# One Trainium2 core, attention and two MLPs: the first tile's output product taken in float32 on whole operands instead of three passes over split operands

## The chip, the core and the metric

The kernel runs on one core of a Trainium2 chip. That core has a matrix engine (TensorE; PE in the rows, with PEld for its weight loads), a vector engine (VectorE, DVE), a scalar engine (ScalarE, ACT), a general engine (GpSimd, POOL) and an engine that here only issues DMAs (SyncE, SP). Each works through its own queue in order, and semaphores tie the queues together. The metric is the device time of one execution in microseconds; lower is better.

## The reference

`reference` computes attention with a feature softmax on q and a sequence softmax on k (8 batches, 8 heads, 576 tokens, head size 64), then a gated MLP, then a second MLP:

```python
q_s = softmax over the head dimension of q
k_s = softmax over the sequence of k
attn = q_s @ (k_s.T @ v)                  # 8 x 8 x 576 x 64 -> x: 4608 x 512
xn = x / rms(x) * rms_g
g, val = xn @ w_gate, xn @ w_val          # 512 -> 1536
y = (silu(g) * val) @ w_out               # 1536 -> 512   <- the product that is changed, for the first 512 tokens
h = y @ w2_in; out = (h * sigmoid(1.702 * h)) @ w2_out    # 512 -> 2048 -> 512
```

q, k, v and rms_g arrive as float32. The five weight matrices arrive as float64 and are turned into float32 on the core.

## The kernel before

**Tiling.** The 4608 tokens are 9 tiles `j` of 512. The hidden width of the first MLP, 1536, is 12 chunks `n` of 128, the model width 512 is 4 chunks `c` of 128. Tile `j` runs through 36 slots, three for each hidden chunk `n`: slot 3n computes the gate product (`hidden`, 12 matmuls, then Silu on ScalarE at L828), slot 3n+1 the value product (`hidden`, 12 matmuls, then the multiplication `s = s * tv` on VectorE at L834), slot 3n+2 the output product `out1` of the chunk before, n-1.

**Split operands.** The products are made of three reduced-precision passes (dtype `float32r`): an operand is split into a high part and a remainder, and `product` (L490) issues high x high, high x low and low x high into the same accumulator. `split_u` (L507) makes the two parts of the gated values with two VectorE instructions, L509 (copy) and L510 (subtract). `split_weight` (L159) makes the two parts of a weight with one ScalarE instruction (L160) and one GpSimd instruction (L161).

**Weights in the first tile.** While tile 0 runs, each slot also calls `advance` once: it decodes one 128 x 512 piece of a float64 weight (ScalarE L148 and L149, VectorE L150, L151 and L154, GpSimd L157) and splits an earlier piece. Pieces of the gate and value weights are kept as their two parts. Pieces of `w_out` are kept whole (`weight["raw", n // 2]`), since they do not fit in both forms; `split_out_weight(n)` splits them again for every tile into a tile `wo`, in tile 0 in slot 3n+2, in the later tiles in slot 3n. The decoding of piece `w_out[n]` stands in slot 3n.

**What sets the order.** All instructions are recorded in program order under a manual schedule, and each engine executes its own in that order. `plan[j][slot]` adds the attention steps of the next tile (`unit_steps`), one unit of two heads every six slots: s0 is the maximum over k (VectorE L316), s1 and s2 transpose it twice on TensorE (L323, L335) with VectorE steps L327, L330, L336 between, s3 is the exponentials (ScalarE L354) and the row sums (VectorE L360 to L362, GpSimd L363), s4 the k-v product in plain float32 (TensorE L370, ten instructions) and its scaling (VectorE L378 to L385), then the q transposes (L399, L407, L408) and the attention products (L414 to L416). In slots 30 to 33 the norm of the next tile is made (`total` L449, `spread` L464, `scale` L470). From tile 1 on no slot calls `advance`.

After the nine tiles follow the two products of the second MLP (L639 and L984), which the change does not touch.

Of the kernel before, what the change touches and what calls it, by code (L numbers as in the profile page):

```python
# [20 lines left out]
def attention_glu_mlp(  # L21
# [26 lines left out]
    nc = tc.nc  # L48
# [4 lines left out]
    P = 128  # L53
# [4 lines left out]
    NC = DM // P  # L58
    NF1 = FF1 // P
# [52 lines left out]
    def f(x):  # L112
        return x.bitcast(F32)
# [51 lines left out]
    weight = {}  # L165
# [51 lines left out]
    def advance(limit=len(todo_pieces)):  # L217


        turn = at["decode"] < limit  # L220
        finish = decode_next() if turn else None
        if at["split"] < at["decode"] - (2 if turn else 0):
            split_next()
        if turn:
            if finish:
                finish()
            fetch_next()
# [3 lines left out]
    def decode_aside():  # L231

        if at["decode"] == len(todo_pieces):
            return
        piece = todo_pieces[at["decode"]]
        decode_next()()
        decoded.append((piece, halves.pop(piece)))
        fetch_next()

    def store_aside():  # L240
        if decoded:
            piece, w32 = decoded.pop(0)
            nc.sync.dma_start(out=w2_d[pieces2.index(piece)], in_=f(w32))
# [3 lines left out]
    def split_out_weight(n):  # L247
        w = sp.tile([P, 2, 512], F32R, tag="wr", bufs=2, name="wo")
        split_weight(w, f(weight["raw", n // 2][:, n % 2, :]))
        wo[n] = w  # L250
# [52 lines left out]
    def bank(tag):  # L303
        bufs = {"att": 2, "gv": 2, "acc": 4}[tag]
        return ps.tile([P, 512], F32, tag=tag, bufs=bufs, name=f"ps_{tag}")
# [175 lines left out]
    def split_x(j, c, side=nc.vector):  # L481
        x = xr.pop((j, c))
        w = sp.tile([P, 2, T], F32R, tag="xs", bufs=4, name="xs")
        nc.scalar.activation(w[:, 0, :], x, AF.Copy)
        side.tensor_tensor(w[:, 1, :], x, f(w[:, 0, :]), op=ALU.subtract)
        xs[j, c] = w
# [3 lines left out]
    def product(t, w, x, first, last):  # L490

        for i, (a, e) in enumerate(PASSES):
            nc.tensor.matmul(t, w(a), x(e), start=first and i == 0, stop=last and i == 2)  # L493

    def hidden(j, w):
        t = bank("gv")
        for c in range(NC):
            product(
                t,
                lambda a, c=c: w[:, a, c * P : (c + 1) * P],  # L500
                lambda e, c=c: xs[j, c][:, e, :],
                c == 0,
                c == NC - 1,
            )
        return t

    def split_u(s):  # L507
        u = sp.tile([P, 2, T], F32R, tag="u", bufs=2, name="u")
        nc.vector.tensor_copy(u[:, 0, :], s)  # L509
        nc.vector.tensor_tensor(u[:, 1, :], s, f(u[:, 0, :]), op=ALU.subtract)  # L510
        return u

    us, acc = {}, {}

    def out1(j, n):
        u, w = us.pop((j, n)), wo.pop(n)
        for c in range(NC):
            if n == 0:
                acc[c] = bank("acc")
            product(  # L520
                acc[c],
                lambda a: w[:, a, c * P : (c + 1) * P],
                lambda e: u[:, e, :],
                n == 0,
                n == NF1 - 1,
            )

    def store_x2(j, c):
        ev = sp.tile([P, T], F32, tag="ev", bufs=2, name="ev")
        nc.scalar.activation(ev, acc[c], AF.Copy)  # L530
        nc.scalar.dma_start(out=x2_d[j][c], in_=ev)
# [16 lines left out]
    def sums(raw, side, engines):  # L548
        for (o, a, b, op), engine in zip(SUMS[side], engines):
            engine.tensor_tensor(raw[:, o], raw[:, a], raw[:, b], op=op)  # L550
# [41 lines left out]
    def pack_steps(kind, q):  # L592
        a, b = (weight_steps(kind, 2 * q + i, nc.gpsimd) for i in range(2))
        return [a[0], b[0], a[1], b[1]] + [x for ab in zip(a[2:], b[2:]) for x in ab]
# [4 lines left out]
    def x2_load(i, c):  # L599
        raw = xraw2[i, c] = raw_tile()  # L600
        for k in range(4):
            done = 0
            while done < W:
                j, o = divmod((2 * i + k % 2) * W + done, T)
                n = min(W - done, T - o)
                nc.sync.dma_start(
                    out=raw[:, k, done : done + n], in_=x2_d[j][c + 2 * (k // 2)][:, o : o + n]
                )
                done += n

    def x2_split(i, p, c):
        pool, tag, bufs = (pools["x"], "xf", 12) if ORDER.index(p) < 5 else (pools["xb"], "xg", 4)
        w = pool.tile([P, 2, W], F32R, tag=tag, bufs=bufs, name=f"xf{p}{c}")
        halve(w[:, 0], w[:, 1], xraw2[i, c][:, RIGHT[p]], nc.vector)
        xfac[i, p, c] = w
# [114 lines left out]
    with tc.manual_schedule():  # L730
# [74 lines left out]
        for j in range(NTILE):  # L805
            if j + 1 == NTILE:

                ap.release()
                pools["raw"] = tc.alloc_tile_pool(name="r2", bufs=1, side="right", reuse_waits="tile")
                pools["x"] = tc.alloc_tile_pool(name="x2p", bufs=1, side="right", reuse_waits="tile")  # L810

                for q, gate in enumerate((10, 20)):
                    steps2 = pack_steps("2i", q)
                    todo += [(gate - 6, fn) for fn in steps2[:4]] + [(gate, fn) for fn in steps2[4:]]
                for c in range(2):
                    todo.append((0, lambda c=c: x2_load(0, c)))
                for c in range(2):
                    todo.append((28, lambda c=c: sums(xraw2[0, c], "B", (nc.vector,) * 4)))
                for p in ORDER[:5]:
                    for c in range(2):  # L820
                        todo.append((0, lambda p=p, c=c: x2_split(0, p, c)))

            for slot in range(SLOTS):
                n, part = divmod(slot, 3)
                if part == 0:
                    tg = hidden(j, weight["g", n])
                    s = sp.tile([P, T], F32, tag="s", bufs=2, name="s")
                    nc.scalar.activation(s, tg, AF.Silu)  # L828
                elif part == 1:
                    tv = hidden(j, weight["v", n])  # L830
                    if n == NF1 - 1 and j + 1 < NTILE:
                        for c in range(NC):
                            split_x(j + 1, c)
                    nc.vector.tensor_tensor(s, s, tv, op=ALU.mult)  # L834
                    us[j, n] = split_u(s)
                    if n == 1 and j:
                        for c in range(2, NC):
                            store_x2(j - 1, c)
                else:
                    if pend:  # L840
                        out1(*pend)
                    if n == 0 and j:
                        for c in range(2):
                            store_x2(j - 1, c)
                    pend = (j, n)
                for fn in plan[j][slot]:
                    fn()
                if part == (2 if j == 0 else 0):
                    split_out_weight(n)
                if j == 0:  # L850
                    advance(len(pieces1))
                elif j + 1 < NTILE:
                    if slot % 6 == 2:
                        decode_aside()
                    elif slot % 6 == 5:
                        store_aside()
                for _ in range(3 if slot < 33 else 2):
                    if todo and todo[0][0] <= slot:
                        todo.pop(0)[1]()
        out1(*pend)  # L860
        for c in range(NC):
            store_x2(NTILE - 1, c)
# [92 lines left out]
        for k in range(NT // T * NSET):  # L955
# [23 lines left out]
            for p in (1, 6, 7, 5, 3, 4, 2):  # L979
                w = wpack["2o", m // 2, p]  # L980
                t = banks[p]
                for i in range(2):
                    for n, (a, e) in enumerate(PASSES):
# [4 lines left out]
                            start=m == 0 and i == 0 and n == 0,  # L988
                            stop=last and n == 2,
# [84 lines left out]
```

## Time and profile before

| what | value |
|---|---|
| time, median of 3 runs | 1816.32 us (1816.26 to 1817.03) |
| time of the profiled execution | 1816.74 us |
| its span, first to last instruction | 1814.9 us |
| busy: PE, DVE, ACT, POOL | 1742.3, 1203.9, 779.9, 396.1 us |
| mean granted TensorE clock | 0.988 |

The span is 1.84 us shorter than the execution's own time; what lies around it is start and end. Shares of busy time are means over stages that have different limits. The first tile lies between about 43 and 204 us of the span; tiles 1 to 8 and then the second MLP fill the rest.

### The profile page before, as it was taken

How to read it: one execution, taken by the hardware profiler on the slowest of the kernel's cores; microseconds unless marked ns; L12 is line 12 of the kernel's file. 1: busy time of each engine (PE TensorE's matmuls, PEld its weight loads, DVE VectorE, ACT ScalarE, POOL GpSimd, SP SyncE). 2: the span in 40 equal slices, each digit the busy share in tenths (PEclk: the TensorE clock that was granted, in tenths of full speed). 3: DMA queues.
4: the chain of work that ended last, by engine and by line, in shares of the span. 5: the costliest groups of instructions: out<-in, count | busy, mean ns of one | idle time of the engine just before them, and what ended most of it. 6: DMA issues, size and time to landing. Idle time of an engine off the chain costs nothing.

```text
span 1814.9 us, 26699 instructions
## 1 busy us (share of the span) xinstructions
PE 1742.3 (96%) x10092; PEld 1543.3 (85%) x10092; DVE 1203.9 (66%) x2017; ACT 779.9 (43%) x1304; POOL 396.1 (22%) x360
## 2 busy tenths in 40 slices
PE   5777999999999999999999999999999999999998
PEld 4565788888888888888888879999999899999998
DVE  7999875775757657575323347556546797777785
ACT  4555544444444444443312236444435543333332
POOL 4666512212121221211111434000002640000000
PEclk9898999999999999999999999999999999999999
DMA  5344341322323232220001015434444544444432
GB/s 156 124 134 127 101 123 55 106 84 67 103 65 105 75 95 75 60 75 20 24 1 47 24 58 186 140 113 141 140 148 159 197 129 139 129 128 128 128 117 82
DMA packets 202001, 186.31 MB, mean 103 GB/s; under 512 B 58256, under 2 KB 183696, under 8 KB 201872
## 3 DMA queue, kind: packets, MB, share of 16 engines
q1 hardware_dynamic: 191888, 166.51, 29.7%
q10 hardware_dynamic: 9984, 18.09, 2.7%
q8 instruction: 79, 1.29, 0.3%
q14 instruction: 50, 0.41, 0.1%
HBM read 119.54 MB, written 65.01 MB: 102 GB/s over the span
## 4 chain that ended last, share of the span: by engine, by line
PE 85%; DVE 10%; issue 2%; DMA 1%; ACT 1%; POOL 0%; SPq 0%; DVEq 0%; ACTq 0%; POOLq 0%
PE ps_gv L493 29%; PE ps_in L639 19%; PE ps_out L984 17%; PE ps_acc L493 15%; PE ps_att L370 1%; PE ps_att L399 1%; DVE uf L722 1%; DVE w L151 1%; DVE raw L151 1%; DVE raw L550 1%; DVE raw L154 1%; DVE u L509 1%; PE ps_att L449 1%; DVE y L998 0%; DVE m L316 0%
## 5 line engine op out<-in xcount | busy, mean ns | idle before, releaser
L984 PE MATMUL ps_out<-w2o,uf 128*128 128x256 f32 x3024 | 366.8, 284 | 5.4 <-DVE uf L722 4.7
L984 PEld LDWEIGHTS ps_out<-w2o,uf 128*128 128x128 f32 x3024 | 365.1, 193 | 7.1 <-DVE uf L722 5.6
L639 PE MATMUL ps_in<-xf,w2i 128*128 128x384 f32 x2016 | 349.9, 334 | 2.4 <-ACT ev L530 2.4
L639 PEld LDWEIGHTS ps_in<-xf,w2i 128*128 128x128 f32 x2016 | 349.4, 188 | 3.1 <-ACT ev L530 2.8
L493 PE MATMUL ps_acc<-u,wo 128*128 128x512 f32 x1296 | 328.6, 403 | 5.7 <-POOL wo L161 5.7
L493 PE MATMUL ps_gv<-xs,wg 128*128 128x512 f32 x1296 | 322.5, 397 | 7.1 <-POOL wg L161 5.6
L493 PE MATMUL ps_gv<-xs,wv 128*128 128x512 f32 x1296 | 319.2, 395 | 0.4 <-DVE s L834 0.4
L493 PEld LDWEIGHTS ps_gv<-xs,wg 128*128 128x128 f32 x1296 | 243.4, 191 | 62.4 <-POOL wg L161 7.7
L493 PEld LDWEIGHTS ps_acc<-u,wo 128*128 128x128 f32 x1296 | 244.9, 193 | 58.6 <-POOL wo L161 6.8
L493 PEld LDWEIGHTS ps_gv<-xs,wv 128*128 128x128 f32 x1296 | 240.6, 189 | 49.4 <-POOL wv L161 1.2
L161 POOL TENSOR_TENSOR wo<-raw,wo 128x512 fp32r<-128x512 f32 x108 | 142.3, 1318 | 495.5 <-ACT wo L160 477.5
L828 ACT ACTIVATE s<-ps_gv 128x512 f32<-128x512 f32 x108 | 64.5, 598 | 428.6 <-PE ps_gv L493 428.6
L834 DVE TENSOR_TENSOR s<-s,ps_gv 128x512 f32<-128x512 f32 x108 | 73.9, 684 | 198.3 <-PE ps_gv L493 174.3
L624 ACT ACTIVATE h<-h 128x384 f32<-128x384 f32 x144 | 74.4, 525 | 115.2 <-DVE h L661 85.1
L157 POOL TENSOR_TENSOR w<-w,stage 128x512 int32<-128x512 int32 x56 | 73.5, 1312 | 220.2 <-DVE w L154 70.9
L550 DVE TENSOR_TENSOR raw<-raw 128x256 f32<-128x256 f32 (+1 forms) x236 | 108.0, 500 | 11.8 <-DMA raw<-w2d 7.6
L661 DVE TENSOR_TENSOR h<-h,ps_in 128x384 f32<-128x384 f32 x144 | 78.0, 553 | 49.8 <-PE ps_in L639 49.3
L719 ACT ACTIVATE uf<-raw 128x1792 fp32r<-128x1792 f32 x36 | 61.2, 1701 | 86.0 <-PE ps_out L984 53.1
L554 POOL TENSOR_TENSOR w2o<-raw,w2o 128x256 fp32r<-128x256 f32 x35 | 28.2, 843 | 275.9 <-DMA u<-h 270.1
L722 DVE TENSOR_TENSOR uf<-raw,uf 128x1792 fp32r<-128x1792 f32 x36 | 74.4, 2067 | 18.7 <-ACT uf L719 18.7
L510 DVE TENSOR_TENSOR u<-s,u 128x512 fp32r<-128x512 f32 x108 | 82.8, 767 | 3.7
L360 DVE TENSOR_REDUCE qs<-qe 128x10 f32<-128x640 f32 x32 | 26.2, 820 | 85.7 <-ACT qe L354 85.6
(139 smaller groups left out, 1863.2 us busy)
## 6 DMA issues: line engine op xcount, KB each, us to landing
u<-h SPq DMA_DIRECT2D x192, 192.0 KB, 1.9
stage<-in_moe_w_out_dram SPq DMA_DIRECT2D x28, 512.0 KB, 3.6
raw<-u SPq DMA_DIRECT2D x24, 512.0 KB, 4.3
x<-ev ACTq DMA_DIRECT2D x36, 256.0 KB, 2.0
stage<-in_moe_w_in_dram SPq DMA_DIRECT2D x16, 512.0 KB, 3.7
w2d<-w SPq DMA_DIRECT2D x32, 256.0 KB, 3.3
v_sb<-in_v_dram SPq DMA_DIRECT2D x60, 128.0 KB, 3.2
out_dram<-y ACTq DMA_DIRECT2D x30, 256.0 KB, 4.3
```

The lines of the kernel that those rows point to most:

```text
L157: return lambda: nc.gpsimd.tensor_tensor(dst, dst, lo, op=ALU.add)
L161: nc.gpsimd.tensor_tensor(dst[:, 1, :], src, f(dst[:, 0, :]), op=ALU.subtract)
L493: nc.tensor.matmul(t, w(a), x(e), start=first and i == 0, stop=last and i == 2)
L510: nc.vector.tensor_tensor(u[:, 1, :], s, f(u[:, 0, :]), op=ALU.subtract)
L550: engine.tensor_tensor(raw[:, o], raw[:, a], raw[:, b], op=op)
L624: nc.scalar.activation(dst, src, AF.Gelu_apprx_sigmoid)
L639: nc.tensor.matmul(t, w[:, a, s, c * P : (c + 1) * P], xfac[i, p, c][:, e, :], start=p in (1, 6, 5) and c == 0 and k == 0, stop=c == 1 and ...
L661: nc.vector.tensor_tensor(v, v, t, op=ALU.add)
L722: nc.vector.tensor_tensor(w[:, 1], raw, f(w[:, 0]), op=ALU.subtract)
L828: nc.scalar.activation(s, tg, AF.Silu)
L834: nc.vector.tensor_tensor(s, s, tv, op=ALU.mult)
L984: nc.tensor.matmul(t[:, i * Q : (i + 1) * Q], u[:, a, LEFT[p] - 1, i * P : (i + 1) * P], w[:, e, m % 2, :], start=m == 0 and i == 0 and n ...
```

## The change

For tile 0 alone, `out1` multiplies the undivided values `s` with the undivided weight piece, viewed as float32, in one matmul instruction for each of the four output chunks. `split_u` is not called for tile 0, and `split_out_weight` is not called in tile 0. Tiles 1 to 8 are as before.

```diff
     def out1(j, n):
+        if j == 0:
+
+            s = us.pop((j, n))
+            w = f(weight["raw", n // 2][:, n % 2, :])
+            for c in range(NC):
+                if n == 0:
+                    acc[c] = bank("acc")
+                nc.tensor.matmul(
+                    acc[c], w[:, c * P : (c + 1) * P], s, start=n == 0, stop=n == NF1 - 1
+                )
+            return
         u, w = us.pop((j, n)), wo.pop(n)
...
-                    us[j, n] = split_u(s)
+                    us[j, n] = split_u(s) if j else s
...
-                if part == (2 if j == 0 else 0):
+                if part == 0 and j:
                     split_out_weight(n)
```

In all it takes 24 instructions off VectorE, 12 off ScalarE and 12 off GpSimd (two, one and one for each hidden chunk), and on TensorE 48 products of three matmuls become 48 of one. Names in the orders below: `raw` is a w_out piece kept whole, `w` a decoded gate or value piece, `wg` and `wv` their split forms, `wo` the split w_out, `u` the split gated values, `xs` the split input; numbers behind them tell buffers apart.

VectorE around the multiplication of chunk 1, in slots 3 and 4 of tile 0. Before:

```order
L150 TENSOR_SCALAR raw_649<-raw_649 128x512
L151 TENSOR_SCALAR raw_649<-raw_649 128x512
L154 SCALAR_TENSOR_TENSOR raw_649<-stage,raw_649 128x512
L834 TENSOR_TENSOR s<-s,ps_gv 128x512
L509 CAST u<-s 128x512
L510 TENSOR_TENSOR u<-s,u 128x512
L378 TENSOR_SCALAR rs<-ps_att 128x1
L379 RECIPROCAL rs<-rs 128x1
```

The same place now:

```order
L154 SCALAR_TENSOR_TENSOR raw_649<-stage,raw_649 128x512
L845 TENSOR_TENSOR s<-s,ps_gv 128x512
L378 TENSOR_SCALAR rs<-ps_att 128x1
L379 RECIPROCAL rs<-rs 128x1
L382 TENSOR_SCALAR kvH_76<-ps_att,rs 64x64 x2
L385 SCALAR_TENSOR_TENSOR kvL_78<-ps_att,rs,kvH_76 64x64 x2
L150 TENSOR_SCALAR w_780<-w_780 128x512
```

The copy and the subtraction behind the multiplication are gone, and the scaling of the k-v product follows it directly.

GpSimd in slots 2 to 4 of tile 0. Before:

```order
L161 TENSOR_TENSOR wv_691<-w_620,wv_691 128x512
L157 TENSOR_TENSOR w_685<-w_685,stage 128x512
L161 TENSOR_TENSOR wo<-raw_649,wo 128x512
L157 TENSOR_TENSOR w_703<-w_703,stage 128x512
L363 TENSOR_TENSOR qe<-qe,qs 128x640
L161 TENSOR_TENSOR wg_748<-w_685,wg_748 128x512
```

The same place now:

```order
L161 TENSOR_TENSOR wv_688<-w_620,wv_688 128x512
L157 TENSOR_TENSOR w_682<-w_682,stage 128x512
L157 TENSOR_TENSOR w_697<-w_697,stage 128x512
L363 TENSOR_TENSOR qe<-qe,qs 128x640
L161 TENSOR_TENSOR wg_742<-w_682,wg_742 128x512
```

The subtraction for `wo` between the last steps of two decodings is gone; nothing else changed places.

TensorE in slots 10 to 12 of tile 0. Before:

```order
L414 MATMUL ps_att<-qH,kvH_76 128x256
L415 MATMUL ps_att<-qL,kvH_76 128x256
L416 MATMUL ps_att<-qH,kvL_78 128x256
L370 MATMUL ps_att<-v_sb_81,ke 64x65 x10
L493 MATMUL ps_acc<-u,wo 128x512 x12
L493 MATMUL ps_gv<-xs,wg_977 128x512 x12
```

The same place now:

```order
L416 MATMUL ps_att<-qH,kvL_78 128x256
L370 MATMUL ps_att<-v_sb_81,ke 64x65 x10
L523 MATMUL ps_acc<-s,raw_834 128x512 x4
L493 MATMUL ps_gv<-xs,wg_943 128x512 x12
```

Twelve split matmuls on `u` and `wo` became four float32 matmuls on `s` and `raw`, at the same place in the queue.

## Rows read from the trace of the kernel before

**Rows 1.** Page: busy time of each engine, and VectorE's busy tenths in 40 slices.

```profile
PE 1742.3 (96%) x10092; PEld 1543.3 (85%) x10092; DVE 1203.9 (66%) x2017; ACT 779.9 (43%) x1304; POOL 396.1 (22%) x360
...
DVE  7999875775757657575323347556546797777785
```

**Rows 2.** Stretches: length, busy us (x instructions) in the order named, clock, DMA, GB/s.

```profile
core 0: us, PE busy (x) PEld busy (x) DVE busy (x) ACT busy (x) POOL busy (x), PEclk, DMA share, GB/s
...
53.40:193.40 140.00, 104.75 (x472) 78.88 (x470) 135.18 (x176) 78.93 (x138) 88.68 (x66) 0.89 0.43 132
...
213.80:323.80 110.00, 109.98 (x571) 89.59 (x569) 72.42 (x134) 51.00 (x87) 23.34 (x18) 1.00 0.28 86
```

**Rows 3.** Line 464, four a tile, whole span and 190 to 330: ns, starts.

```profile
L464 PE MATMUL ps_att<-ident,rms x36: 271/272/476, 43.1 to 973.5; 128*128 128x128 f32 x36
...
L464 PE MATMUL ps_att<-ident,rms x8: 271/272/273, 203.8 to 315.9; 128*128 128x128 f32 x8
```

**Rows 4.** Waits from 53.4 to 193.4: total us, times, longest.

```profile
PE ps_att L323 <- DVE qL L408: 16.3, 3, 5.8
...
PE ps_acc L493 <- POOL wo L161: 5.7, 2, 4.0
...
DVE qs L360 <- ACT qe L354: 1.0, 1, 1.0
```

**Rows 5.** Chain of waits at tile 0's end: start, us, engine, tile, line.

```profile
193.42 0.69 DVE sqa L444
...
194.15 1.87 PE ps_att L449 x8
196.02 5.22 PE ps_gv L493 x12
201.25 2.73 PE ps_acc L493 x12
```

**Rows 6.** VectorE's groups from 53.4 to 193.4: busy us, mean ns.

```profile
L510 DVE TENSOR_TENSOR u<-s,u 128x512 fp32r<-128x512 f32 x10 | 12.8, 1276 | 0.3
...
L509 DVE CAST u<-s 128x512 fp32r<-128x512 f32 x10 | 10.3, 1027 | 0.3
```

**Rows 7.** The same lines after 230 us: ns, smallest, median, largest.

```profile
L509 DVE CAST u<-s x73: 426/427/429, 230.9 to 897.1; 128x512 fp32r<-128x512 f32 x73
...
L510 DVE TENSOR_TENSOR u<-s,u x73: 691/693/694, 231.4 to 897.5; 128x512 fp32r<-128x512 f32 x73
...
L151 DVE TENSOR_SCALAR w<-w x31: 426/427/429, 241.5 to 800.0; 128x512 int32<-128x512 int32 x31
```

**Rows 8.** Timeline, VectorE and GpSimd at 64 and 72 us: start, duration.

```profile
64.06 1.49 POOL L161 TENSOR_TENSOR wo<-raw,wo 128x512 fp32r<-128x512 f32 x1
...
64.43 1.40 DVE L151 TENSOR_SCALAR w<-w 128x512 int32<-128x512 int32 x1
...
72.87 1.03 DVE L509 CAST u<-s 128x512 fp32r<-128x512 f32 x1
...
73.58 1.48 POOL L161 TENSOR_TENSOR wv<-w,wv 128x512 fp32r<-128x512 f32 x1
...
73.94 1.67 DVE L510 TENSOR_TENSOR u<-s,u 128x512 fp32r<-128x512 f32 x1
```

**Rows 9.** GpSimd's group of w_out splits from 53.4 to 193.4.

```profile
L161 POOL TENSOR_TENSOR wo<-raw,wo 128x512 fp32r<-128x512 f32 x9 | 13.2, 1464 | 0.0
```

**Rows 10.** Timeline of TensorE: start, duration, instruction records merged.

```profile
83.28 5.34 PE L493 MATMUL ps_acc<-u,wo 128*128 128x512 f32 x12
...
212.60 2.88 PE L493 MATMUL ps_gv<-xs,wg 128*128 128x512 f32 x12
215.32 2.88 PE L493 MATMUL ps_gv<-xs,wv 128*128 128x512 f32 x12
...
226.68 0.95 PE L370 MATMUL ps_att<-v_sb,ke 128*64 128x65 f32 x20
227.56 3.02 PE L493 MATMUL ps_acc<-u,wo 128*128 128x512 f32 x12
...
309.26 0.95 PE L449 MATMUL ps_att<-ones,sqa 128*128 128x1 f32 x8
310.07 2.29 PE L493 MATMUL ps_gv<-xs,wv 128*128 128x512 f32 x9
```

## The prediction

> **What bounds the kernel now.** I read the page first: TensorE is busy 96% of the span, but VectorE's slices show nines near the start, where the first tile lies [rows 1]. So I asked for stretches. From 53.4 to 193.4 us, inside tile 0, VectorE is busy 135.18 of 140 us (97%), TensorE 104.75 at a mean granted clock of 0.89; one tile later, from 213.8 to 323.8 us, TensorE is busy 109.98 of 110 us at clock 1.00 and VectorE 72.42 [rows 2]. The limit changes from VectorE to TensorE between the two. Line 464 stands in one place of every tile (four matmuls, 36 in nine tiles) and works as a ruler: from 43.1 to 203.8 us is tile 0, 160.7 us; from 203.8 to 973.5 us there are seven more tiles, 110.0 us each [rows 3]. Tile 0 thus lasts 50.7 us longer than TensorE alone would need for the same work, and that is the most that relief of VectorE could bring. The waits agree: in this stretch TensorE waits 16.3 us for VectorE's L408 at L323 and 5.7 us for GpSimd's split of `wo`, while VectorE waits 1.0 us in all for anybody [rows 4]. The chain of waits runs through VectorE up to L444 at 193.42 us, goes over to TensorE's L449 at 194.15, and stays on TensorE [rows 5]. What VectorE loses or gains before 193.4 us moves the end of the kernel one to one; what happens behind it counts on TensorE.
>
> **What the change takes away.**
>
> *VectorE's splits.* In the VectorE-bound stretch stand 10 pairs of L509 and L510, 10.3 + 12.8 = 23.1 us [rows 6]. But the same instructions take 0.427 and 0.693 us after 230 us [rows 7], so 10 x 1.12 = 11.2 us of that is their own work and 11.9 us is something else. The timeline shows what: L510 starts at 73.94, while GpSimd's L161 runs from 73.58 to 75.06, and ends at 75.61, 0.55 us behind it; L509 and L151 show the same pattern [rows 8]. VectorE stands still while GpSimd works. The 11.2 us are safe, with 20 gaps of about 0.03 us that go too: 0.6 us (between 72.87 + 1.03 and 73.94 lie 0.04 us [rows 8]). Of the 11.9 us, that part goes which does not reappear at the next VectorE instruction. Behind the multiplication now stand steps that read PSUM or reduce (L378 to L385 in one chunk, L408, L327, L330 in the other), some 1.5 us in each, and they were not slowed in the trace beside GpSimd; then L150 comes, which is slowed. Bounds 0 and 11.9; I take half, 5.9.
>
> *GpSimd's splits of `wo`.* Nine stand in the stretch, 13.2 us [rows 9]. None is on the path itself, but the L151 beside the one at 64.06 is 1.40 us long instead of 0.427 [rows 7, 8]: 0.97 us, and nine times that, if the others delay VectorE alike, is 8.7 us. In GpSimd's new order nothing moves up into the place, since what follows is a decoding step that waits for VectorE's own L154. Bounds 0 (the delay reappears later) and 8.7; I take 8.7, as the row shows the pair. ScalarE's 12 instructions cost and bring nothing: ScalarE is busy 78.93 of 140 us.
>
> The Trainium skill, SBUF — State Buffer, in the section with the single rule on contention, calls the pair of ports that VectorE and GpSimd share an exclusive lock, held for a whole instruction; [rows 8] agree with their 0.55 us. [...]
>
> **What the change adds.** TensorE gets float32 matmuls of 512 columns, and the trace has none. Today's price of a product: 12 split matmuls from 212.60 to 215.32 us, 0.227 us each, three to a product, 0.68 us [rows 10]. The trace has float32 matmuls of 65 columns: L370 stands ten times in a unit and shows 20 records, so one instruction is two records, and the 20 take 0.88 us to the next start, 0.044 us each [rows 10]. It also has L449 with one column: 8 records in 0.81 us, 0.10 us each, which is what a record costs with almost nothing to stream [rows 10]. Lower bound: a record costs what a split matmul costs, 2 x 0.227 = 0.45 us. Upper bound: the two heads of L370, which write different halves of the bank, ran side by side, and 65 columns take 0.088 us: 1.35 ns a column, 0.69 us a record, 1.39 us a product. I take L370 as it stands, 0.68 ns a column, 0.35 us, and add the 0.10 us of L449: 0.45 us a record, **0.90 us a product**, 0.22 more than now. In tile 0's 48 products this is 10.6 us more TensorE work: 110.0 + 10.6 = 120.6 us, below the 134 us or so that VectorE will still need. This cover hides it up to 193.4 us. Behind that it is exposed: the products of chunks 9, 10 and 11 come after L449 [rows 5], 12 x 0.22 = 2.7 us lost (bounds: 2.8 gained, 8.5 lost).
>
> The Trainium skill, FP8 and Floating Point Precision, TensorE Precision Notes, says that true float32 makes four passes through the array. By that rule an estimate is 4 x 0.227 = 0.91 us a product and the sum stays within 0.1 us of mine; no run here shows it yet.
>
> *The clock.* After the wait for L408 the 12 matmuls at 83.28 us took 5.34 us, against 2.72 at full clock [rows 10]; at tile 0's end the value product behind L449 took 5.22 us, also at the lower of the two levels (1.2 instead of 2.4 GHz) [rows 5]. With less waiting for VectorE the second could be at the full level: 0 to 2.5 us gained on the path, I take 1.2.
>
> *New waits.* VectorE must still wait for ScalarE's exponentials before L360, which come behind a gate product and Silu. Today that is 1.0 us in all [rows 4]; with VectorE earlier it will be more. Five units lie in tile 0; I put 1 us in all, bounds 0 and 5. No new wait on buffers arises: `s` has two buffers and is now read by TensorE as late as the next-but-one gate product, but the Silu that overwrites it stands behind that product anyway. `raw` is ready five slots before it is read.
>
> **The sum.** 11.2 + 0.6 + 5.9 + 8.7 = 26.4 us off VectorE's path; less 2.7 and 1, plus 1.2: 23.9 us. The profiled execution took 1816.74 us, so 1792.8; the median of the runs is 0.42 us lower, which gives **1792.4 us**.
>
> **The rivals.**
>
> *The blocked time moves on.* GpSimd's remaining steps block VectorE just as long as today: only 11.2 + 0.6 us of the splits go, and of the 8.7 us half. 11.8 + 4.3 - 2.7 - 1 + 0.6 = 13 us, 1803 us. For it: L151 is slowed almost wherever it stands. Against: the steps behind the multiplication now are of the kinds that are not slowed.
>
> *VectorE's relief is complete and more.* All 11.9 us go, and TensorE no longer falls to the lower level: 11.8 + 11.9 + 8.7 - 2.7 + 2.5 = 32 us, 1784 us; the end of this line is 50.7 - 10.6 = 40 us, where TensorE is the limit, 1776 us.
>
> *TensorE becomes the bound of tile 0.* At the upper price, 1.39 us, it has 110.0 + 48 x 0.71 = 144 us, tile 0 shrinks by 16.7 us at most, and with hand-overs between the engines that are no longer hidden I give it 5 to 10 us: about 1809 us.
>
> *No change.* VectorE's time in tile 0 isn't the limit but only stretched work, and the chain closes over ScalarE and GpSimd: 1816 us. Against it stands VectorE's 1.0 us of waiting.
>
> *Slower: the float32 products hold TensorE at its lower level.* The place is `out1` in every chunk of tile 0. At that level a pass takes 5.34 / 12 = 0.445 us [rows 10]; four of them, which is what my 0.90 us amounts to at full level, 1.78 us, so a chunk costs 4 x 1.10 = 4.4 us more, and the product behind it 2.5 us more, as at 196.02 us [rows 5]. It decides from 50.7 / 12 = 4.2 us more per chunk; at 6.9 us tile 0 gets 32 us longer: 1848 us. Against it: the clock is at 1.00 wherever TensorE is kept busy [rows 2], and these products keep it busy longer.
>
> **How the numbers follow.** Forecast (gain of 18 to 30 us) 0.55; blocked time moves on (10 to 18 us) 0.18; complete relief (30 to 40 us) 0.11; TensorE the bound (4 to 10 us) 0.06; no change 0.05; slower 0.05. A measurement of this kernel can tell 0.2%, 3.6 us, from no change. Faster 0.90, same 0.05, slower 0.05. The range takes the forecast, most of the first rival (down to a gain of 12 us) and the near part of complete relief (up to 33 us): 1783.5 to 1804.5 us.
>
> **What would show it.** Right: between 53 and some 168 us VectorE stays busy above 90%, without L509 and L510, L151 often at 0.43 us; line 464 of tile 0 comes near 180 us; tiles 1 to 8 keep 110.0 us; a float32 product group of four takes 3.6 us at full clock. Wrong: the group takes over 5.6 us; L151 stays at 1.4 us and L150 grows (the first rival); VectorE waits for PSUM at its multiplication (TensorE the bound); the granted clock in tile 0 falls below 0.89 (slower).

## The result and the profile after

The changed kernel takes **1789.05 us** (median of 4 runs, 1787.73 to 1789.49) against 1816.29 (4 runs, 1816.07 to 1817.03): ratio 0.9845, 95% interval 0.9833 to 0.9856, 27.2 us less. Predicted were 1792.4 us and a range of 1783.5 to 1804.5. The profiled execution took 1789.49 us, with a span of 1787.7; the difference of the two profiled spans is 27.2 us too.

First the ruler, line 464, whole span and around tile 0's end (durations in ns, first and last start), beside [rows 3]:

```profile
L464 PE MATMUL ps_att<-ident,rms x36: 271/272/475, 42.9 to 944.7; 128*128 128x128 f32 x36
...
L464 PE MATMUL ps_att<-ident,rms x4: 272/272/273, 173.0 to 173.4; 128*128 128x128 f32 x4
```

Tile 0 lasts from 42.9 to 173.0, 130.1 us instead of 160.7. From this mark to the last one, seven tiles on, pass 771.7 us instead of 769.7, 110.2 us a tile instead of 110.0. So the whole gain arises in tile 0: 30.8 us up to this mark. At the last mark 28.8 us are left (944.7 against 973.5), at the end 27.2.

Then the stretch of tile 0 (length, busy us and instructions of PE, PEld, DVE, ACT and POOL, granted clock, DMA share, GB/s), beside [rows 2]:

```profile
53.40:165.80 112.40, 101.04 (x435) 66.38 (x434) 107.72 (x157) 72.06 (x126) 74.04 (x57) 0.97 0.53 163
```

VectorE is still busy 107.72 of 112.4 us (96%): it remains the limit, with less to do. TensorE is busy 90% of the stretch, at a granted clock of 0.97 instead of 0.89. The waits of both in that stretch (total us, times, longest), beside [rows 4]:

```profile
PE ps_att L323 <- DVE qL L408: 6.0, 3, 2.5
PE ps_att L335 <- DVE m L327: 4.1, 3, 2.6
...
DVE qs L360 <- ACT qe L354: 1.6, 2, 1.1
```

TensorE's wait at L323 fell from 16.3 to 6.0 us, the one for `wo` is gone, and VectorE waits 1.6 us instead of 1.0 us.

The price of the float32 products stands in two views: the durations of their records in ns, and TensorE's timeline (start, duration) at the end of tile 0:

```profile
L523 PE MATMUL ps_acc<-s,raw x96: 590/592/1061, 65.0 to 191.7; 128*128 128x512 f32 x96
...
188.70 3.60 PE L523 MATMUL ps_acc<-s,raw 128*128 128x512 f32 x8
192.14 0.27 PE L335 MATMUL ps_att<-ident,m 128*128 128x128 f32 x1
```

48 instructions are 96 records, two each, as with L370. From the group's start to the next instruction's start, 188.70 to 192.14, pass 3.44 us: 0.43 us a record, 0.86 us a product, against 0.68 for three split matmuls.

Last, the chain of waits at tile 0's end (start, us, engine, tile, line), beside [rows 5]:

```profile
164.45 1.33 DVE sqa L444
165.78 1.44 DVE w L150
...
172.78 1.65 DVE raw L154
...
174.50 0.70 POOL raw L157
...
175.78 1.48 POOL wv L161
...
177.30 2.56 PE ps_gv L493 x10
179.87 3.43 PE ps_acc L523 x8
```

L444, where the chain left VectorE before, now starts at 164.45 instead of 193.42, 29.0 us earlier. But the chain does not leave there any more: it stays on VectorE up to 174.4 us, goes over two GpSimd instructions, the end of a decoding (L157) and the split of a value weight (L161), and reaches TensorE only at 177.30.

### The profile page after: what moved, and what is told of

Its sections match the earlier page's. It is cut to its first block, busy times and chain, and to the rows that moved or that the text cites. A ratio compares the mean times of both kernels' runs of the same rounds, so it can differ in the third digit from the quotient of the medians.

```text
span 1787.7 us, 26545 instructions
## 1 busy us (share of the span) xinstructions
PE 1737.2 (97%) x10044; PEld 1525.4 (85%) x10044; DVE 1173.7 (66%) x1993; ACT 773.5 (43%) x1292; POOL 376.2 (21%) x348
## 4 chain that ended last, share of the span: by engine, by line
PE 88%; DVE 9%; issue 1%; DMA 1%; ACT 1%; POOL 0%; DVEq 0%; SPq 0%; ACTq 0%
PE ps_gv L493 30%; PE ps_in L650 19%; PE ps_out L995 19%; PE ps_acc L493 15%; PE ps_att L370 1%; PE ps_att L399 1%; DVE w L151 1%; DVE uf L733 1%; DVE raw L151 1%; DVE w L154 1%; PE ps_acc L523 1%; DVE w L150 1%; DVE raw L154 1%; DVE m L316 0%; PE ps_att L449 0%
## 5 line engine op out<-in xcount | busy, mean ns | idle before, releaser
L493 PE MATMUL ps_acc<-u,wo 128*128 128x512 f32 x1152 | 283.3, 395 | 0.0
L493 PEld LDWEIGHTS ps_acc<-u,wo 128*128 128x128 f32 x1152 | 212.4, 188 | 44.3
L161 POOL TENSOR_TENSOR wo<-raw,wo 128x512 fp32r<-128x512 f32 x96 | 124.0, 1292 | 499.0 <-ACT wo L160 486.6
L157 POOL TENSOR_TENSOR w<-w,stage 128x512 int32<-128x512 int32 x56 | 73.3, 1309 | 214.5 <-DVE w L154 65.6
L565 DVE TENSOR_TENSOR xf<-raw,xf 128x384 fp32r<-128x384 f32 x84 | 43.8, 567 | 47.0 <-ACT xf L564 47.0
```

The costliest lines, as they stand in the source:

```text
L157: return lambda: nc.gpsimd.tensor_tensor(dst, dst, lo, op=ALU.add)
L161: nc.gpsimd.tensor_tensor(dst[:, 1, :], src, f(dst[:, 0, :]), op=ALU.subtract)
L565: engine.tensor_tensor(dst_l, src, f(dst_h), op=ALU.subtract)
```

## Experiments

Two theories stood against each other: that tile 0 lasts as long as VectorE's queue, made up of its own work and of the time in which GpSimd holds it up; and that the gain comes from TensorE's side, from no waiting for `wo` and from a higher clock.

**All splits kept, unread.** In the slot loop of the changed kernel:

```diff
+                    if j == 0:
+                        split_u(s)
                     us[j, n] = split_u(s) if j else s
...
-                if part == 0 and j:
+                if part == (2 if j == 0 else 0):
                     split_out_weight(n)
```

> The first tile multiplies whole operands in float32 as in the change, but VectorE still makes the two parts of every s and ScalarE and GpSimd still split w_out; nobody reads them. Theory (tile 0 lasts as long as VectorE's queue, and float32 on TensorE alone brings nothing): VectorE has its old queue, so the 1816.3 us of before, plus three exposed float32 groups of 0.73 us: 1816 to 1820 us. Rival (the gain comes from TensorE's side: no waiting for wo, a higher granted clock since the longer products keep it busy): most of the gain stays, at or below 1805 us.

Measured: 1818.23 us (1816.76 to 1820.23), ratio to the kernel before 1.0009, interval 0.9999 to 1.0018. Its stretch in tile 0:

```profile
53.40:193.00 139.60, 108.90 (x438) 69.77 (x436) 135.79 (x176) 79.88 (x139) 88.64 (x66) 0.90 0.43 132
```

VectorE is busy 97%, as before, and the clock is 0.90 in the mean of the stretch, against 0.89: float32 on TensorE alone brings no time, although nothing waits for `wo` any more. The rival on TensorE's side falls.

**Each half of the splits kept alone.** The first with only the second hunk of the diff above, the second with only the first.

> The change, but ScalarE and GpSimd still split w_out in tile 0; nobody reads the result. Theory (each GpSimd split holds up a VectorE instruction beside it for 0.97 us, nine of them on the path): 8.7 us of the gain are lost, 1796 to 1799 us against 1789.05. Rival (the blocked time is always taken up by the next VectorE instruction, whatever GpSimd does): at most 4 us lost, 1789 to 1793 us.

> The change, but VectorE still makes the two parts of s in tile 0; nobody reads them. Theory (the pair's own 1.12 us ten times, 0.6 us of gaps, and half of the 11.9 us in which GpSimd held it up): 17.7 us lost, 1805 to 1809 us. Rival (its blocked time moved on to the next instruction in the change, so that only its own work came off): 11.8 us lost, 1800 to 1802 us. Rival (all of it came off): 23.7 us lost, 1811 to 1814 us.

Measured: keeping the splits of `w_out` 1796.09 us (1795.82 to 1797.91), 7.0 us of the gain lost, where 8.7 was predicted; keeping those of `s` 1810.45 us (1810.29 to 1811.01), 21.4 us lost, between the 17.7 of the theory and the 23.7 for which all the blocked time had to come off, and in neither range. (The 1789.05 us of the changed kernel are those of the result, with the kernel before at 1816.29; beside these runs it took 1816.56.) Together 28.4 us; with both kept the kernel above lost 29.2 us, so the two halves add up within the noise. Line 151 tells which half does what. Its rows for the gate and value pieces in tile 0 (ns, smallest, median, largest; from 53.4 us to 193.4, 165.8, 185 and 185), of the kernel before, the changed one, the one with the `w_out` splits kept and the one with the splits of `s` kept:

```profile
L151 DVE TENSOR_SCALAR w<-w x18: 426/1370/1420, 59.7 to 183.6; 128x512 int32<-128x512 int32 x18
```

```profile
L151 DVE TENSOR_SCALAR w<-w x18: 426/428/1416, 57.8 to 158.2; 128x512 int32<-128x512 int32 x18
```

```profile
L151 DVE TENSOR_SCALAR w<-w x20: 426/1383/1418, 57.6 to 176.4; 128x512 int32<-128x512 int32 x20
```

```profile
L151 DVE TENSOR_SCALAR w<-w x18: 426/428/1421, 59.2 to 175.7; 128x512 int32<-128x512 int32 x18
```

With GpSimd's split of `w_out` in the queue the median is 1.37 or 1.38 us, without it 0.428, whatever VectorE does with `s`. An L151 that is slowed loses 0.95 us, but by the run time the nine splits cost 7.0 us, 0.78 us each: some of the lost time would have been lost elsewhere. The run keeps ScalarE's copies for `wo` together with GpSimd's subtractions and does not part the two; the timeline does. In tile 0 of these kernels L151 takes 1.36 us or more wherever it overlaps a GpSimd instruction and 0.43 us wherever it does not.

**The relief without float32.** In the kernel before, tile 0 splits only its first chunk's values and `w_out` piece, and multiplies those in all twelve chunks; the other splits of tile 0 are left out:

```diff
-                    us[j, n] = split_u(s)
+                    us[j, n] = us_first if j == 0 and n else split_u(s)
+                    if j == 0 and n == 0:
+                        us_first = us[j, n]
...
-                    split_out_weight(n)
+                    if j == 0 and n:
+                        wo[n] = wo_first
+                    else:
+                        split_out_weight(n)
+                        if j == 0:
+                            wo_first = wo[n]
```

> The kernel before, in which tile 0 makes the parts of s and of w_out for its first hidden chunk only and multiplies those in all twelve; the splits of the other eleven chunks are left out, so the first tile's result is another. It has the relief of VectorE and GpSimd without the float32 matmuls. Theory (float32 is hidden behind VectorE up to the norm of tile 1 and exposed in three groups of 0.73 us): 2.2 us faster than the change, give or take the first chunk's splits, 1786 to 1789 us. Rival (the float32 price is on the path in all twelve chunks, 8.8 us): 1779 to 1782 us.

Measured: 1789.02 us (1788.28 to 1790.01), the time of the change. The theory's 2.2 us of advantage did not show, but it had left the first chunk's splits open: the one remaining pair on VectorE and one split on GpSimd are worth some 3 us by the runs above (28.4 / 10 on the path). Its L449 stands at 168.8 us instead of 165.9; at tile 8's mark 1.6 us of that are left (946.3 against 944.7). Cheaper products thus gave back about 1.3 us and no more. The rival, by which float32 costs 8.8 us in tile 0, falls: VectorE hides nearly all of it.

**Float32 in tile 1 as well** (`j < 2` in place of `j == 0` in the three places).

> The change in tile 0 and in tile 1 as well. Tile 1 is bound by TensorE, so its 48 float32 products lie on the path and show their price, while the splits that go with them there bring nothing. Theory (a group of four takes 3.45 us to the end of its last record, as the chain of the changed kernel has it, against 2.72 for twelve split matmuls): 12 x 0.73 = 8.8 us slower than the change, 1797 to 1799 us. The predicted 0.90 us a product would give 10.6 us, 1799.6 us. Rival (the price is what lies between the starts of a group and of the one after it, 3.03 us): 3.7 us, 1792.8 us.

Measured: 1797.05 us (1795.57 to 1798.06), against 1788.74 (1786.74 to 1789.96) for the changed kernel run again on the same chip:

> The changed kernel again, beside the others on the same chip: 1788 to 1790 us.

The difference, 8.3 us, is 0.69 us a chunk and 0.17 a product: 0.85 us for a float32 product where nothing hides it. The theory said 8.8; the rival's 3.7 us falls. In tile 1, where TensorE is the limit, the same edit that won 27 us in tile 0 loses 8.

**Gate and value weights split on VectorE.** If GpSimd's instructions cost VectorE that much, the other splits should move too:

```diff
-    def split_weight(dst, src):
+    def split_weight(dst, src, engine=nc.gpsimd):
         nc.scalar.activation(dst[:, 0, :], src, AF.Copy)
-        nc.gpsimd.tensor_tensor(dst[:, 1, :], src, f(dst[:, 0, :]), op=ALU.subtract)
+        engine.tensor_tensor(dst[:, 1, :], src, f(dst[:, 0, :]), op=ALU.subtract)
...
-        split_weight(w, f(halves.pop(piece)))
+        split_weight(w, f(halves.pop(piece)), nc.vector)
```

> The change, with the subtractions for the gate and value weights moved from GpSimd to VectorE (24, of which some 20 lie on VectorE's path in tile 0). Theory (a GpSimd split holds VectorE up for about as long as VectorE would need for it: the nine for w_out cost 7.0 us when they were kept, 0.78 us each, and VectorE's own subtraction takes 0.69 us and 0.03 us of gap): 20 x (0.72 - 0.78) = -1 us, 1786 to 1791 us against 1789.05. Rival (GpSimd's splits of gate and value weights mostly stand beside steps that they do not hold up): up to 14 us slower, 1797 to 1803 us.

> The kernel with the subtractions for gate and value weights on VectorE again, beside the one above on the same chip: 1784 to 1786 us.

Measured: 1784.88 us (1784.38 to 1785.75) and, again, 1784.25 (1781.68 to 1784.98): 3.9 us faster than the 1788.74 us of the changed kernel beside the first. VectorE got 24 instructions more and the kernel became faster, by more than the 1 us of the theory and below its range. Its groups from 53.4 to 160 us (busy us, mean ns):

```profile
L154 DVE SCALAR_TENSOR_TENSOR w<-stage,w 128x512 int32<-128x512 int32 x18 | 12.5, 692 | 0.6
...
L151 DVE TENSOR_SCALAR raw<-raw 128x512 int32<-128x512 int32 x10 | 9.1, 914 | 0.3
...
L154 DVE SCALAR_TENSOR_TENSOR raw<-stage,raw 128x512 int32<-128x512 int32 x10 | 6.9, 693 | 0.3
L161 DVE TENSOR_TENSOR wg<-w,wg 128x512 fp32r<-128x512 f32 x10 | 6.8, 684 | 0.0
```

and the same lines of the changed kernel, from 53.4 to 165.8 us:

```profile
L154 DVE SCALAR_TENSOR_TENSOR w<-stage,w 128x512 int32<-128x512 int32 x18 | 16.4, 909 | 0.6
...
L151 DVE TENSOR_SCALAR raw<-raw 128x512 int32<-128x512 int32 x10 | 13.9, 1391 | 0.3
...
L154 DVE SCALAR_TENSOR_TENSOR raw<-stage,raw 128x512 int32<-128x512 int32 x10 | 11.7, 1170 | 0.3
```

L154 fell to its undisturbed 0.69 us in all 28 instances, 8.7 us in all; L151 lost 7.3 us (28.3 to 21.0 with the gate and value pieces), L150 and L444 about 2. Against these 18 us stand some 19 subtractions of 0.68 us that VectorE took on, with their gaps 13.5 us. The theory had counted only what a split of `w_out` had cost. The chain changes too: in this kernel it leaves VectorE at 142.56 us and runs on TensorE from there, 35 us earlier than in the changed kernel.

```profile
141.90 0.61 DVE wv L161
142.56 2.57 PE ps_gv L493 x10
```

**The last two chunks split.** Chunks 10 and 11 of tile 0 as before the change (`j == 0 and n < 10` for the float32 branch), first alone, then together with the weights' splits on VectorE:

> The change for chunks 0 to 9 of tile 0; chunks 10 and 11, whose products come after VectorE's stretch, are split as before. Theory (two float32 groups of 0.73 us come off TensorE's path and the splits are hidden there): 1.5 us faster than the change, 1787 to 1789 us. Rival (VectorE is still on the path when it makes the parts of chunk 10): same or up to 2 us slower.

> The subtractions of gate and value weights on VectorE, and chunks 10 and 11 split. Splitting the last two chunks alone cost 2.2 us, with VectorE still on the path when it made the parts of chunk 10. With the weights' subtractions off GpSimd, the chain runs on TensorE from 142 us on. Theory (what failed there was VectorE's queue and nothing else, so here the two float32 groups of 0.73 us come off TensorE's path): 1783 to 1784 us, against 1784.88 with the subtractions moved alone. Rival (the splits at the tile's end cost what they cost there wherever VectorE stands): 1786 to 1788 us.

Measured: alone 1790.95 us (1789.6 to 1791.78), 2.2 us slower than the changed kernel on the same chip; together 1781.92 us (1780.11 to 1783.27), 2.3 us faster than 1784.25 beside it and below the theory's range. In both pairs the intervals against the kernel before overlap (in the second 0.9804, from 0.9789 to 0.9818, and 0.9814, from 0.9797 to 0.9830). The ruler is sharper, since it leaves out what comes behind the nine tiles, which no edit touches. Line 464 of the changed kernel run again, of the first, and then of the second and of the kernel beside it:

```profile
L464 PE MATMUL ps_att<-ident,rms x36: 271/272/476, 43.1 to 944.8; 128*128 128x128 f32 x36
```

```profile
L464 PE MATMUL ps_att<-ident,rms x36: 271/272/476, 43.0 to 945.4; 128*128 128x128 f32 x36
```

```profile
L464 PE MATMUL ps_att<-ident,rms x36: 271/272/476, 42.6 to 936.9; 128*128 128x128 f32 x36
```

```profile
L464 PE MATMUL ps_att<-ident,rms x36: 271/272/475, 43.2 to 938.8; 128*128 128x128 f32 x36
```

The first comes 0.6 us later at the last mark, not 2.2. In the second, 1.3 us less pass from tile 0's mark (167.4 and 168.0) to the last one: 769.5 against 770.8, close to the 1.5 us of two float32 groups. The chain of the first shows why it did not gain:

```profile
174.46 0.61 DVE s L845
175.09 1.07 DVE u L509
176.18 1.66 DVE u L510
...
179.45 1.31 POOL raw L157
180.75 1.25 POOL wo L161
...
182.05 2.60 PE ps_acc L493 x10
```

VectorE and GpSimd are still on the path when they make the parts of chunk 10, and TensorE goes on with its product at 182.05, where the float32 product stood at 179.87: 2.2 us later, of which the two cheaper products give 1.4 back. Where the chain had left VectorE at 142 us, the same edit came out on the other side. The last kernel is the fastest of all, 35.6 us below the 1817.56 us of the kernel before beside it.

## Why the prediction was right

**The limit.** That tile 0 is bound by VectorE held: keeping VectorE's and GpSimd's instructions, with float32 products, gave 1818.23 us, and only tile 0 became shorter. The rival "no change" falls with it.

**The terms on VectorE.** Predicted were 26.4 us off VectorE's path, less 1 us of new waits; L444 starts 29.0 us earlier. The term that was mis-sized is the half of the 11.9 us of blocked time. Keeping the splits of `s` cost 21.4 us; less 11.8 for their own work and gaps, 9.6 us of the blocked time had come off, not 5.9. Part of that is the tile's end; read at L444, which starts last at 184.7 us there (the row below) and at 164.4 in the changed kernel, it is 20.3 - 11.8 = 8.5 us.

```profile
L444 DVE TENSOR_TENSOR sqa<-sqa,sqb x3: 679/693/694, 132.5 to 184.7; 128x512 f32<-128x512 f32 x3
```

The reason given for the half was that steps which read PSUM or reduce are not slowed beside GpSimd. The kernel before hardly showed it for the steps named: L327, L330 and L378 to L385 never overlap a GpSimd instruction in its tile 0 (at 75.53 us, behind the L510 of [rows 8], GpSimd has been idle since 75.06); only half of the L408 do. The choice of a half was thus in part a guess. The changed kernel shows it, VectorE and GpSimd at 69 us (start, duration):

```profile
69.48 1.32 POOL L157 TENSOR_TENSOR raw<-raw,stage 128x512 int32<-128x512 int32 x1 [0.63 <-DVE raw L154]
...
70.30 0.60 DVE L382 TENSOR_SCALAR kvH<-ps_att,rs 64x64 fp32r<-64x64 f32 x2
...
70.76 1.29 POOL L161 TENSOR_TENSOR wv<-w,wv 128x512 fp32r<-128x512 f32 x1
...
70.93 0.60 DVE L385 SCALAR_TENSOR_TENSOR kvL<-ps_att,rs,kvH 64x64 fp32r<-64x64 f32 x2
71.56 0.77 DVE L150 TENSOR_SCALAR w<-w 128x512 f32<-128x512 f32 x1
```

L378 to L385, L327, L330 and L408 now overlap GpSimd every time and keep the durations of before. They fill most of the time in which GpSimd works after a multiplication, so little moves on. It did move on in part, to L150; its rows before and now:

```profile
L150 DVE TENSOR_SCALAR w<-w 128x512 f32<-128x512 f32 x18 | 10.4, 576 | 0.1
```

```profile
L150 DVE TENSOR_SCALAR w<-w 128x512 f32<-128x512 f32 x19 | 12.9, 678 | 0.1
```

The splits of `w_out` brought 7.0 us instead of 8.7. The first rival (everything blocked moves on, 1803 us) falls with this. The Trainium skill, SBUF — State Buffer, in its section Who interferes with whom, calls the shared ports an exclusive lock, but says that reductions, and VectorE instructions with at most one input from SBUF outside the two-port modes, do not contend with GpSimd. These rows agree: what the lock costs hangs on which instruction stands next.

**The price of float32.** 0.86 us in the chain and 0.85 from tile 1, against my 0.90 from two rows of small matmuls; the bounds 0.45 and 1.39 held. That 0.90 came so near is in part luck: a whole record of L370 takes 0.044 us, less than the 0.10 of L449 that was added as what every record costs. The cover in tile 0 held (1.3 us came back without float32). The estimate from the four passes that the Trainium skill, FP8 and Floating Point Precision, TensorE Precision Notes, states was 0.91 us; the measured 0.85 to 0.86 us is 6% below it.

**The tile's end.** Here a step failed, without much effect on the sum. I let the chain go over to TensorE at L449, as before, and counted the products of chunks 9, 10 and 11 as exposed (2.7 us lost) with 1.2 us back from the clock. In the changed kernel VectorE and GpSimd hold the chain until 177.30 us, so the product of chunk 9 is covered and only the last two are exposed, 2 x 0.72 = 1.4 us; splitting those two alone gained nothing, as shown. TensorE did come to its full level: the value product behind L449 takes 2.85 us from start to next start (166.75 to 169.60) instead of 5.22 us, and L449 itself 0.89 instead of 1.87. That is 3.3 us where 1.2 was put, though not all on the path. In the kernel with the relief alone the two take 3.75 us together, as in the change (3.74), so less waiting is enough for it, as predicted; with all splits kept it was 5.3. Between tile 0's mark and the last one 2.0 us were lost, of which the two products are 1.4. The mark itself was predicted near 180 us and came at 173.0: the gain up to there was larger than predicted, and the total of 1792.4 us lies so near also because 3.6 us were lost behind the mark, of which the prediction had only two products, 1.8 us.

**What stays open.** Behind the last mark another 1.6 us were lost in the profiled execution (843.0 us against 841.4), in stages that the change does not touch. In the profile of the changed kernel's repetition the same part takes 840.9 us, and over the twelve profiles of this case it lies between 840.9 and 844.5. So the 1.6 us lie within the spread between executions; where that spread comes from is open.

**The other rivals.** "Slower" needed a lower clock during the float32 products: in the mean of the stretch it was 0.97. Single groups did run slower, the one at 77.14 us behind a wait for L408 took 5.1 us to the next start instead of 3.4, but VectorE never waited for TensorE in the stretch. "TensorE becomes the bound" needed 1.39 us a product. Both fall with the rows above.

## To carry to other kernels

Ask of each stage which engine is never idle there: the same edit, more matrix work for fewer vector instructions, won 27 us in the tile that VectorE bounds and lost 8 in the next one that TensorE bounds. When an instruction takes two or three times its undisturbed duration, look at what runs beside it: an instruction on an engine that is off the path can be worth half of its own length (0.78 us for a split of 1.46 us here). And after a relief find out anew where the chain changes engines, before refining anything behind that point.

## What the runs showed of the hardware

- A float32 matmul of 128 x 512 is two records of 0.43 us, 0.86 us in a stream, where one split pass takes 0.227 us: three split passes are cheaper than one float32 instruction by 0.17 to 0.18 us.
- In the stretch of tile 0, before and after, L151 takes 1.36 to 1.44 us when it overlaps a GpSimd instruction and 0.43 us when it does not, L154 1.63 to 1.67 against 0.69; L378 to L385, L327, L330 and L408 take the same either way.
- Moving 24 subtractions from GpSimd (1.3 to 1.5 us each) to a VectorE that was 96% busy made the kernel 3.9 us faster. GpSimd is held up in turn: its L157 on the `raw` pieces, each of which starts while a subtraction runs on VectorE, takes 1.63 us in the mean there, against 1.30 in the changed kernel, and that subtraction keeps its 0.68 us.

```profile
L157 POOL TENSOR_TENSOR raw<-raw,stage 128x512 int32<-128x512 int32 x10 | 16.3, 1631 | 13.9 <-ACT w L148 6.4 <-ACT stage L149 5.2 <-issue 1.1
```
